# Exact-part value products and block-by-block order in the first batch of a fused attention and SwiGLU kernel

## The chip, the cores and the metric

The kernel runs on one core of one Trainium2 chip. The metric is the device time of one execution in microseconds. A profile of one execution gives the busy time of each engine, the waits, and the chain of work that ended last. PE is TensorE (matrix products), PEld its weight loads, DVE is VectorE, ACT is ScalarE, POOL is GpSimd and SP is SyncE, which issues DMA transfers here.

## The reference

Polynomial-sketch attention is followed by a SwiGLU feed-forward block. Cut to what matters:

```python
# q, k, v: (4, 4, 1088, 32); S1, S2: (8, 32)
def phi(x):
    a = np.einsum('rd,bhsd->bhsr', S1, x)
    b = np.einsum('rd,bhsd->bhsr', S2, x)
    return np.einsum('bhsi,bhsj->bhsij', a, b).reshape(*x.shape[:-1], 64)
q_p, k_p = phi(q), phi(k)
kv = np.einsum('bhsf,bhsd->bhfd', k_p, v)
z = np.sum(k_p, axis=2)
num = np.einsum('bhsf,bhfd->bhsd', q_p, kv)
den = np.einsum('bhsf,bhf->bhs', q_p, z)[..., None] + 1e-06
x = (num / den).transpose(0, 2, 1, 3).reshape(4352, 128)

# w_gate, w_val: (128, 1536); w_out: (1536, 128)
g = x @ w_gate
out = (g / (1 + np.exp(-g)) * (x @ w_val)) @ w_out
```

## The kernel before

The 4352 tokens are cut into blocks. The first batch of attention (1088 tokens) makes blocks 0, 1 and 2, of 384, 384 and 320 tokens; the rest of the tokens are in blocks of 480, and a last one of 384. The hidden dimension of 1536 is cut into 12 chunks of 128. One unit (block i, chunk j) is a gate product, a value product, and the hidden tile, silu(gate) times value. A down product then multiplies the hidden tile with a chunk of `w_out` into an accumulating bank of PSUM. The schedule is written out by hand: the order in which Python calls the helpers is the order in every engine's queue.

There are two kinds of unit. `unit` makes both products in plain fp32 (line 1015): ScalarE applies Silu to the gate bank (L1019), and VectorE multiplies with the value bank into the hidden tile (L1030). For the first six units (`late`), ScalarE only copies the value product, and the multiplication is done later by GpSimd, in `catch_up` (L1036).

`cut_unit` makes the value product, and in a later stretch the gate product too, out of parts in F32R. A weight w is cut into `w1` (w scaled by CUT and rounded to F32R, by ScalarE), `low` (w minus w1, subtracted by GpSimd or VectorE), `wb` (low times BETA, by ScalarE) and `wd` (w1 minus wb, or the same from low). Tokens are cut in the same way, into `x1`, `x0` and `xd`, by `cut_tokens` (L875, L876, L880). Three F32R products take the place of one fp32 product: wd with xd in one bank (L968), and w1 with x1 plus wb with x0 in another (L978, L979). ScalarE copies the first one to SBUF with a factor (`sums`, L972), VectorE combines it with the second bank (L980), and GpSimd multiplies the result with silu(gate) into the hidden tile (L991). Before the change only blocks from 3 on go this way; the parts of `wv` are made by `cut_weights` near the end of the first batch.

The first batch's main loop goes through `seq`, a list of 30 units; z is the position in it. At fixed positions it calls other steps:

- `parts` converts weights. The weights come as 64-bit words, and `narrow` turns each piece of three chunks into fp32 in three steps: step 1 on VectorE (L256, L257), step 2 on ScalarE (L261, L262), step 3 on VectorE (L264, L270) and GpSimd (the product in L279). Piece 3 is chunks 6 to 8 and piece 4 chunks 9 to 11. For piece 4 step 3 of `wg` is at z=8 and that of `wv` at z=10. The four pieces of `wo` have step 3 at z=14, 16, 20 and 22.
- From z=17 on, each position also has one down product (L1060) and one step of the generator `attentions`, which prepares the second batch of attention: transposes of keys and queries, key products (L347), key features (L370), the sums of features on GpSimd (`feature_sums`, L540, issued at z=24), and at z=26 `values`: the key values (L381) and a product of ones with the feature sums (L713).
- At z=24, 25 and 26 `catch_up` multiplies the last three late units.

PSUM has eight banks. Units take single banks in turn from `free_banks`, four at first, and three from z=17 on, since one accumulates the down products. A plain unit takes two banks. Hidden tiles go to `slots`: 27 tiles of 384 columns, in `hbuf` (17) and `late` (10). A down product gives its slot back. After the first batch `hbuf` is divided anew, into 13 slots of 480 columns; the rest of `late` serves for parts of the gate weights and for key features.

After the loop the remaining down products follow, with the rest of the second batch's attention among them; then the numerators (L776) and the second loop, over y, with blocks from 3 on.

Of the kernel before, what the change touches and what calls it, by code (L numbers as in the profile page):

```python
# [7 lines left out]
FP32 = mybir.dt.float32  # L8
# [11 lines left out]
def kernel(  # L20
# [279 lines left out]

    NH = 27
    NL = 10
    hbuf = const.tile([P, NH - NL, BW], FP32, name="hbuf")
    late = const.tile([P, NL, BW], FP32, tag="late", name="late", bufs=1)
    slots = [(hbuf[:, k, :] if k < NH - NL else late[:, k - NH + NL, :]) for k in range(NH)]
    slot_of = {}

    xT = const.tile([P, NT], FP32, name="xT")  # L310
# [297 lines left out]
    def attentions():  # L608
# [28 lines left out]
            f()  # L637
        yield from turn_keys(2)
        kvz = wide("a")
        values(kvz[:, 0, :], phk, zs)  # L640
        kab, kcopies = sketched(wide("b"), key_products, 2, "kab2")
        fold(kvz[:, 0, :])
        spread = spread_out(1, kvz[:, 0, :])
        hold("a", "b")
# [21 lines left out]
        for b in (2, 3):  # L666
            yield "pe"
            if b == 3:
                numerators(2, spread)
            hold("a")  # L670
            kv = bank()
            kv_bank = [max(used, key=used.get)]
            release("a")
            values(kv, phk, zs)
            if b == 2:
                kab, copies = sketched(wide("a"), key_products, 2, "kab2")
                run_copies(copies, 2)
            fold(kv)
            spread = spread_out(b, kv)
            touch(*kv_bank)  # L680
            yield
            yield "pe"
            qab, copies = sketched(wide("b"), query_sketches, 3, "qab")
            run_copies(copies, 2)
            yield
            if b == 2:
                yield from turn_queries(3)
                phk = late[:, NL - 6 :, :].rearrange("p s (n h i j) -> p (s n) h i j", h=1, i=R, j=R)
# [20 lines left out]
    def values(kv, phk, zs):  # L709

        key_values(kv[:, 0:F], phk, 0, NC)
        for h in range(H):
# [105 lines left out]
    def homes(w):  # L818


        if w is wv:
            for c in range(4):
                yield [
                    stage.tile([P, 3, P], F32R, tag=tag, name=name, bufs=6)[:]
                    for tag, name in (("exp", "w1"), ("man", "wb"), (("exp", "man")[c % 2], "wd"))
                ]
        else:
            big = lambda pool, tag, bufs: pool.tile([P, 2, 3, P], F32R, tag=tag, name="g" + tag, bufs=bufs)
            for c in range(2):
                t = [big(stage, "raw", NRAW), big(stage, "raw", NRAW), big(apool, "phq", 2)]  # L830
                for k in range(2):
                    yield [x[:, k] for x in t]

    def cut_weights(w, lows, engine):

        rows = [], [], [], []
        sub = dict(op=ALU.subtract)
        for c, (w1, wb, wd) in enumerate(homes(w)):
            src = w[:, 3 * c : 3 * c + 3, :]
            low = lows[c]  # L840
            w_parts[id(w), c] = (w1, wb, wd)
            fine = dict(out=wd, in0=whole(w1), in1=whole(wb), **sub), engine.tensor_tensor
            if engine is nc.vector:
                fine = dict(
                    out=wd, in0=low, scalar=-BETA, in1=whole(w1), op0=ALU.mult, op1=ALU.add
                ), engine.scalar_tensor_tensor
            for row, f, args in zip(
                rows,
                (nc.scalar.activation, engine.tensor_tensor, nc.scalar.activation, fine[1]),
                (  # L850
                    dict(out=w1, in_=src, func=AF.Copy, scale=CUT),
                    dict(out=low, in0=src, in1=whole(w1), **sub),
                    dict(out=wb, in_=low, func=AF.Copy, scale=BETA),
                    fine[0],
                ),
            ):
                row.append((f, args))
        return rows

    def take(steps, n):  # L860

        for _ in range(n):
            if steps:
                f, args = steps.pop(0)
                f(**args)

    def cut_tokens(i, engine=nc.gpsimd):

# [404 lines left out]
            parts.setdefault(at, []).append(p)  # L1273
    seq = [(0, 3), (0, 4), (0, 5), (2, 0), (2, 1), (2, 2)]
    seq += [(i, j) for i in (1, 2) for j in range(3, 6)]
    seq += [(i, j) for j0 in (6, 9) for i in range(3) for j in range(j0, j0 + 3)]
    order = [(i, j) for i in range(3) for j in range(NCH)]
    for z, (i, j) in enumerate(seq):
        if z == 17:
            free_banks.pop()  # L1280
            turn[0] %= 4
        unit(i, j)
        for p in parts.get(z, ()):
            part(*p)
        if z in (24, 25, 26):
            catch_up()
        if z == 6:
            load_k(1)
# [2 lines left out]
        if z >= 17:  # L1291
            todo.remove(order[0])
            todo.insert(0, order.pop(0))
            down()
        if z == 20:
            lows = [
                pool.tile([P, 3, P], FP32, tag=tag, name="low", bufs=bufs)[:]
                for pool, tag, bufs in ((apool, "qb", 2), (apool, "dT", 2), (apool, "rd", 2), (apool, "qb", 2))
            ]
            first, low, second, third = cut_weights(wv, lows, nc.gpsimd)  # L1300
        if z in (20, 21):
            take(first, 2)
        if z == 21:
            take(low, 3)
        if z == 25:
            take(second, 3)
        if z >= 17:
            parts_of(1)
        if z == 26:
            take(low, 1)  # L1310
            take(third, 3)
        if z == 29:
            take(second, 1)
            take(third, 1)
    todo.sort()
    x_steps = None
    while todo:
# [7 lines left out]
        parts_of(1)  # L1325
    run(x_steps or cut_tokens(HEAD, nc.vector))

    flat = hbuf[:].rearrange("p s w -> p (s w)")
    slots[:] = [flat[:, WB * k : WB * k + WB] for k in range((NH - NL) * BW // WB)]

# [13 lines left out]
    gate_rows = []  # L1344
    down_steps = cut_down()
    for y in range(END):
        i, j = line[y // NCH], y % NCH
# [1 line left out]
            group()  # L1349
        if y == GATES:  # L1350
            hold("g2")
        if y == END - 1:
            finish()
            unit(i, j)
        else:
            cut_unit(i, j, both=y >= GATES, y=y)
# [3 lines left out]
                down(y)  # L1360
        parts_of(y < GATES or y % 2 == 0)
        if y == 0:
            gate_rows = cut_weights(wg, lows, nc.vector)
        for n, row in enumerate(gate_rows):
            if y >= (0, 2, 6, 6)[n]:
                take(row, 1)
        for gen in token_steps.get(y, ()):
            next(gen, None)
        if y in range(24, 38, 2):
# [44 lines left out]
```

## Time and profile before

| | before |
|---|---|
| device time, median of 3 runs | 285.89 us (285.68 to 286.83) |
| span of the profile | 283.9 us, 5583 instructions |
| granted TensorE clock | 1.00 |
| HBM read and written | 11.41 and 2.23 MB |

The profile's shares by stretch, from the windows view (busy us of each engine):

| stretch, us | length | PE | DVE | ACT | POOL | what runs |
|---|---|---|---|---|---|---|
| 26.5 to 36.6 | 10.1 | 10.10 | 9.24 | 5.48 | 5.22 | z=0 to 7 |
| 36.6 to 49.5 | 12.9 | 12.90 | 10.69 | 7.99 | 3.10 | z=8 to 17 |
| 49.5 to 63.4 | 13.9 | 13.90 | 11.70 | 7.20 | 7.06 | z=18 to 23 |
| 63.4 to 77.5 | 14.1 | 14.10 | 7.09 | 5.57 | 10.82 | z=24 to 29 |
| 77.5 to 93.2 | 15.7 | 15.24 | 11.82 | 1.30 | 1.36 | down products, query features |

A busy time of PE is that of matmul records, whose ends are modelled and which overlap, so it says when TensorE had something in work and not how fast it went. For that the starts of successive matmuls in the timeline are read. The times of a line with "<-" are idle time of that engine just before the operation, and what ended it.

### The profile page before, as it was taken

What the parts mean: (1) busy time and instruction counts of PE and PEld (TensorE: products, weight loads), DVE (VectorE), ACT (ScalarE), POOL (GpSimd) and SP (SyncE); (2) the same over time, 40 slices, a digit from 0 to 9 for tenths busy, and PEclk for the clock granted to TensorE, in tenths of its full rate; (3) what the DMA queues carried; (4) which work ended last, traced back from release to release, by engine and by line L of the source; (5) the groups of instructions that cost most, each with busy time, mean ns of one, the idle gap of its engine ahead of it and who ended that gap; (6) DMA issues with size and microseconds to landing.
All of it is one profiled execution on the core that took longest, in us unless ns stands there. A gap on an engine that the chain in (4) does not pass through costs nothing.

```text
span 283.9 us, 5583 instructions
## 1 busy us (share of the span) xinstructions
PE 276.7 (97%) x2129; PEld 190.9 (67%) x2129; DVE 221.0 (78%) x324; ACT 175.5 (62%) x316; POOL 177.3 (62%) x173
## 2 busy tenths in 40 slices
PE   8899999999999999999999999999999999999995
PEld 7545565666656576555576677657777777778984
DVE  3997988975495986999648898749889969988741
ACT  3558665633401756645366777867888888977850
POOL 3314432279500896489935787659889889878660
PEclk9999999999999999999999999999999999999999
DMA  7574193222231123000100020001000200010021
GB/s 196 156 225 111 48 288 124 81 78 81 67 56 28 27 89 86 2 0 11 28 16 0 0 36 2 0 2 27 8 0 1 37 0 0 11 27 1 0 34 28
DMA packets 26138, 14.28 MB, mean 50 GB/s; under 512 B 19840, under 2 KB 24192, under 8 KB 26112
## 3 DMA queue, kind: packets, MB, share of 16 engines
q1 hardware_dynamic: 25456, 13.84, 18.7%
q8 instruction: 16, 0.26, 0.4%
q10 hardware_dynamic: 656, 0.10, 0.2%
q14 instruction: 10, 0.08, 0.1%
HBM read 11.41 MB, written 2.23 MB: 48 GB/s over the span
## 4 chain that ended last, share of the span: by engine, by line
PE 86%; DVE 6%; DMA 3%; ACT 2%; issue 1%; SPq 0%; DVEq 0%; ACTq 0%
PE PS L1060 24%; PE PS L1015 16%; PE PS L968 11%; PE PS L978 10%; PE PS L979 10%; PE PS L970 5%; DMA vld<-in_v_dram 2%; PE PS L776 2%; PE PS L335 2%; DMA raw<-in_moe_w_val_dram 1%; PE PS L347 1%; DVE sum L980 1%; PE PS L1088 1%; PE PS L1055 1%; PE PS L1052 1%
## 5 line engine op out<-in xcount | busy, mean ns | idle before, releaser
L991 POOL TENSOR_TENSOR hbuf<-sg,sum 128x480 f32<-128x480 f32 (+1 forms) x83 | 104.9, 1269 | 36.9 <-ACT sg L986 29.3
L980 DVE SCALAR_TENSOR_TENSOR sum<-PS,sum 128x960 f32<-128x960 f32 (+2 forms) x83 | 83.3, 1004 | 27.7 <-ACT sum L972 21.6
L972 ACT ACTIVATE sum<-PS 128x960 f32<-128x960 f32 (+2 forms) x83 | 70.9, 854 | 39.3 <-PE PS L968 37.9
L1060 PE MATMUL PS<-hbuf,wo 128*128 128x480 f32 (+3 forms) x142 | 57.5, 505 | 0.0
L968 PE MATMUL PS<-xd,gphq 128*128 128x480 f32 (+1 forms) x63 | 40.0, 636 | 0.5 <-DVE xd L880 0.5
L978 PE MATMUL PS<-x,w 128*128 128x480 f32 (+1 forms) x83 | 38.5, 464 | 0.0
L986 ACT ACTIVATE sg<-sum 128x480 f32<-128x480 f32 (+1 forms) x63 | 36.6, 581 | 1.0 <-DVE sum L980 0.9
L968 PE MATMUL PS<-xd,wd 128*128 128x480 f32 (+1 forms) x83 | 35.8, 432 | 0.5 <-DVE xd L880 0.5
L1060 PEld LDWEIGHTS PS<-hbuf,wo 128*128 128x128 f32 x142 | 26.6, 189 | 8.4 <-issue 0.9
L979 PE MATMUL PS<-x,wb 128*128 128x480 f32 (+1 forms) x83 | 31.2, 376 | 0.0
L1015 PE MATMUL PS<-xT,wg 128*128 128x384 f32 (+1 forms) x74 | 29.5, 480 | 0.1
L1015 PE MATMUL PS<-xT,wv 128*128 128x384 f32 (+1 forms) x74 | 28.8, 471 | 0.2 <-DVE wv L279 0.2
L1019 ACT ACTIVATE sg<-PS 128x384 f32<-128x384 f32 (+1 forms) x31 | 14.4, 467 | 21.3 <-PE PS L1015 19.6
L968 PEld LDWEIGHTS PS<-xd,wd 128*128 128x128 f32 x83 | 15.7, 189 | 13.1 <-issue 11.8
L978 PE MATMUL PS<-x,graw 128*128 128x480 f32 (+1 forms) x63 | 23.5, 373 | 0.2 <-ACT xT L793 0.2
L979 PE MATMUL PS<-x,graw 128*128 128x480 f32 (+1 forms) x63 | 23.3, 370 | 0.0
L1060 PE MATMUL PS<-hbuf,scaled 128*128 128x480 f32 x48 | 23.2, 564 | 0.0
L1015 PEld LDWEIGHTS PS<-xT,wv 128*128 128x128 f32 x74 | 13.8, 190 | 9.2 <-DVE hbuf L1030 0.9
L968 PEld LDWEIGHTS PS<-xd,gphq 128*128 128x128 f32 x63 | 11.9, 188 | 11.7 <-issue 6.8
L1015 PEld LDWEIGHTS PS<-xT,wg 128*128 128x128 f32 x74 | 13.3, 189 | 9.4 <-issue 1.3
L978 PEld LDWEIGHTS PS<-x,w 128*128 128x128 f32 x83 | 15.6, 188 | 5.8 <-issue 3.4
L979 PEld LDWEIGHTS PS<-x,wb 128*128 128x128 f32 x83 | 15.6, 188 | 5.7 <-issue 4.3
(173 smaller groups left out, 457.6 us busy)
## 6 DMA issues: line engine op xcount, KB each, us to landing
kld<-in_k_dram SPq DMA_DIRECT2D x4, 544.0 KB, 4.1
vld<-in_v_dram SPq DMA_DIRECT2D x12, 144.0 KB, 4.8
qld<-in_q_dram SPq DMA_DIRECT2D x3, 544.0 KB, 3.3
raw<-in_moe_w_out_dram SPq DMA_DIRECT2D x4, 384.0 KB, 3.7
raw<-in_moe_w_gate_dram SPq DMA_DIRECT2D x3, 384.0 KB, 3.2
raw<-in_moe_w_val_dram SPq DMA_DIRECT2D x3, 384.0 KB, 3.6
out_dram<-o SPq DMA_DIRECT2D x16, 60.0 KB, 2.0
vld<-in_v_dram SPq DMA_DIRECT2D x4, 112.0 KB, 4.5
```

Of the source, the lines that this page charges most:

```text
L335: nc.tensor.matmul(ps[32 * a : 32 * a + 32, 96 * (c - c0) : 96 * (c - c0) + 96], qT[:, 4 * c + a, :], s123[:, a : a + H, :, :].rearrange(" ...
L968: nc.tensor.matmul(ds[:, k], wd, xd, start=True, stop=True)
L970: nc.tensor.matmul(g, wg[:, j, :], xT[:, t0 : t0 + n], start=True, stop=True)
L972: nc.scalar.activation(sums, ds, AF.Copy, scale=-1.0 / BETA)
L978: nc.tensor.matmul(ps[:, k], w1, x1, start=True, stop=False)
L979: nc.tensor.matmul(ps[:, k], wb, x0, start=False, stop=True)
L980: nc.vector.scalar_tensor_tensor(out=sums, in0=ps, scalar=1.0 + 1.0 / BETA, in1=sums, op0=ALU.mult, op1=ALU.add)
L986: nc.scalar.activation(sg, sums[:, 0] if both else g, AF.Silu)
L991: nc.gpsimd.tensor_tensor(out=hj[:, 0:n], in0=sg, in1=sums[:, len(ws) - 1], op=ALU.mult)
L1015: nc.tensor.matmul(o[:, 0:n], w[:, j, :], xT[:, t0 : t0 + n], start=True, stop=True)
L1019: nc.scalar.activation(sg[:, 0:n], g[:, 0:n], AF.Silu)
L1060: nc.tensor.matmul(acc[i][:, 0:n], w, hidden[i, j][:, 0:n], **sides)
```

## The change

From chunk 6 on the three blocks of the first batch are gone through one after the other (block 0's chunks 6 to 11, then block 1's, then block 2's), instead of three chunks of each block in turn. The twelve units of blocks 1 and 2 (z=18 to 29) then become cut units, whose value products are made of exact parts[...].

For that the parts of `wv`'s chunks 6 to 11 are made at z=11 to 16 instead of from z=20 on, and those of chunks 0 to 5 at z=20 to 27; the tokens of blocks 1 and 2 are cut at z=13 to 19. The three late catch-ups move from z=24 to 26 to z=8 to 10. `cut_weights` with its rows becomes `cut_chunk`, a generator for one group of three chunks. The parts find room in other tiles; the slots go from 27 to 24, in three tiles, of which `more` also holds the key features of the third batch and gives slots back to the second loop from y=20 on. After the first batch `hbuf` has 11 slots of 480 columns. In the second batch's attention `values` is split, so that the key products of the next batch come ahead of the product with the feature sums.

The core of the diff:

```diff
-    NH = 27
+    NH = 24
     NL = 10
     hbuf = const.tile([P, NH - NL, BW], FP32, name="hbuf")
-    late = const.tile([P, NL, BW], FP32, tag="late", name="late", bufs=1)
-    slots = [(hbuf[:, k, :] if k < NH - NL else late[:, k - NH + NL, :]) for k in range(NH)]
+    late = const.tile([P, 4, BW], FP32, tag="late", name="late", bufs=1)
+    more = const.tile([P, NL - 4, BW], FP32, name="more")
+    slots = [t[:, k, :] for t, n in ((hbuf, NH - NL), (late, 4), (more, NL - 4)) for k in range(n)]
...
         kvz = wide("a")
-        values(kvz[:, 0, :], phk, zs)
+        key_values(kvz[:, 0, 0:F], phk, 0, NC)
         kab, kcopies = sketched(wide("b"), key_products, 2, "kab2")
+        value_sums(kvz[:, 0, :], zs)
         fold(kvz[:, 0, :])
...
+    def cut_chunk(w, home, low, engine):
+
+        c, (w1, wb, wd) = home
+        src = w[:, 3 * c : 3 * c + 3, :]
+        nc.scalar.activation(w1, src, AF.Copy, scale=CUT)
+        yield
+        engine.tensor_tensor(out=low, in0=src, in1=whole(w1), op=ALU.subtract)
+        yield
+        nc.scalar.activation(wb, low, AF.Copy, scale=BETA)
+        yield
+        if engine is nc.vector:
+            engine.scalar_tensor_tensor(
+                out=wd, in0=low, scalar=-BETA, in1=whole(w1), op0=ALU.mult, op1=ALU.add
+            )
+        else:
+            engine.tensor_tensor(out=wd, in0=whole(w1), in1=whole(wb), op=ALU.subtract)
+        w_parts[id(w), c] = w1, wb, wd
+        yield
...
-    seq += [(i, j) for j0 in (6, 9) for i in range(3) for j in range(j0, j0 + 3)]
+    seq += [(i, j) for i in range(3) for j in range(6, NCH)]
...
+    CUTS = 18
...
     for z, (i, j) in enumerate(seq):
         if z == 17:
             free_banks.pop()
             turn[0] %= 4
-        unit(i, j)
+        if z == CUTS:
+            turn[0] = 1
+        if z < CUTS:
+            unit(i, j)
+        else:
+            cut_unit(i, j)
         for p in parts.get(z, ()):
             part(*p)
-        if z in (24, 25, 26):
+        if z in (8, 9, 10):
             catch_up()
...
+        if z == 11:
+            give(cut_chunk(wv, next(home_v), room_for(fpool, "o", 2), nc.gpsimd), 11, 12, 14, 15)
+            give(cut_chunk(wv, next(home_v), room_for(fpool, "o", 2), nc.gpsimd), 12, 13, 15, 16)
+            give(cut_tokens(1), 13, 15)
+            give(cut_tokens(2), 16, 19)
         if z == 20:
...
+            lows = [room_for(fpool, "o", 2) for _ in range(2)]
+            give(cut_chunk(wv, next(home_v), lows[0], nc.gpsimd), 20, 21, 25, 26)
+            give(cut_chunk(wv, next(home_v), lows[1], nc.gpsimd), 21, 22, 26, 27)
         if z >= 17:
             parts_of(1)
...
+        for gen in steps_at.get(z, ()):
+            next(gen, None)
```

The first of the two chunk groups that are cut at z=11 holds chunks 9 to 11, the second chunks 6 to 8. The numbers behind each `give` are the positions of the generator's successive steps.

More of the change, by code (lines that the diff above doesn't have):

```diff
@@ L687, in attentions @@
                 yield from turn_queries(3)
-                phk = late[:, NL - 6 :, :].rearrange("p s (n h i j) -> p (s n) h i j", h=1, i=R, j=R)
+                phk = more[:].rearrange("p s (n h i j) -> p (s n) h i j", h=1, i=R, j=R)
                 phk = phk.rearrange("p (c h) o i j -> p c (h o) i j", h=H)
@@ L711, in values, with value_sums @@
         key_values(kv[:, 0:F], phk, 0, NC)
+        value_sums(kv, zs)
+    def value_sums(kv, zs):
         for h in range(H):
@@ L818, in homes @@
     def homes(w):
+        room = lambda tag, bufs: lambda: stage.tile([P, 3, P], F32R, tag=tag, name="w" + tag, bufs=bufs)[:]
+        big = lambda pool, tag, bufs: pool.tile([P, 2, 3, P], F32R, tag=tag, name="w" + tag, bufs=bufs)
+        exp, man = room("exp", 6), room("man", 6)
         if w is wv:
[L822 to L826, printed above, removed]
-        else:
[L828 to L865, printed above, removed]
+            x, y = (big(apool, "phq", 2) for _ in range(2))
+            yield 3, [x[:, 0], x[:, 1], y[:, 0]]
+            x = const.tile([P, 3, 3, P], F32R, name="w2")
+            yield 2, [x[:, k] for k in range(3)]
+            yield 0, [exp(), man(), exp()]
+            yield 1, [exp(), man(), man()]
+        else:
+            for c in range(NCH // 3):
+                x = big(stage, "raw", NRAW)
+                yield c, [x[:, 0], x[:, 1], (exp, man)[c % 2]()]
@@ L1275, with give @@
     seq += [(i, j) for i in (1, 2) for j in range(3, 6)]
-    seq += [(i, j) for j0 in (6, 9) for i in range(3) for j in range(j0, j0 + 3)]
+    seq += [(i, j) for i in range(3) for j in range(6, NCH)]
     order = [(i, j) for i in range(3) for j in range(NCH)]
+    home_v = homes(wv)
+    room_for = lambda pool, tag, bufs: pool.tile([P, 3, P], FP32, tag=tag, name="low", bufs=bufs)[:]
+    CUTS = 18
+    steps_at = {}
+    def give(gen, *at):
+        for z in at:
+            steps_at.setdefault(z, []).append(gen)
     for z, (i, j) in enumerate(seq):
@@ L1294 @@
             down()
-        if z == 20:
[L1296 to L1306, printed above, removed]
+        if z == 11:
[3 more added lines that the diff above has]
+            give(cut_tokens(2), 16, 19)
+        if z == 20:
+            lows = [room_for(fpool, "o", 2) for _ in range(2)]
+            give(cut_chunk(wv, next(home_v), lows[0], nc.gpsimd), 20, 21, 25, 26)
+            give(cut_chunk(wv, next(home_v), lows[1], nc.gpsimd), 21, 22, 26, 27)
         if z >= 17:
             parts_of(1)
[L1309 to L1314, printed above, removed]
+        for gen in steps_at.get(z, ()):
+            next(gen, None)
     todo.sort()
@@ L1326, with wide_slots @@
     run(x_steps or cut_tokens(HEAD, nc.vector))
-    flat = hbuf[:].rearrange("p s w -> p (s w)")
-    slots[:] = [flat[:, WB * k : WB * k + WB] for k in range((NH - NL) * BW // WB)]
+    def wide_slots(t, n):
+        flat = t[:].rearrange("p s w -> p (s w)")
+        return [flat[:, WB * k : WB * k + WB] for k in range(n * BW // WB)]
+    slots[:] = wide_slots(hbuf, NH - NL)
     END = len(line) * NCH
@@ L1343 @@
     lows = [late[:, c, :].rearrange("p (c f) -> p c f", f=P) for c in range(4)]
-    gate_rows = []
+    gate_steps = []
     down_steps = cut_down()
@@ L1351 @@
             hold("g2")
+            slots += wide_slots(more, NL - 4)
         if y == END - 1:
@@ L1362 @@
         if y == 0:
[L1363 to L1366, printed above, removed]
+            gate_steps = [cut_chunk(wg, h, low, nc.vector) for h, low in zip(homes(wg), lows)]
+        for k, gen in enumerate(gate_steps):
+            for at in (0, 2, 6, 6):
+                if y == at + k:
+                    next(gen)
         for gen in token_steps.get(y, ()):
```

## The prediction

> **What bounds the kernel now.** I read the page first, then the chain of waits, then the timelines of all engines between 26 and 96 us, where the change lies.
>
> ```profile
> PE 276.7 (97%) x2129; PEld 190.9 (67%) x2129; DVE 221.0 (78%) x324; ACT 175.5 (62%) x316; POOL 177.3 (62%) x173
> PE 86%; DVE 6%; DMA 3%; ACT 2%; issue 1%; SPq 0%; DVEq 0%; ACTq 0%
> ```
>
> TensorE sets the time: 86% of the chain that ended last. A busy share of 97% alone would not prove it, so I looked at its timeline around the changed stretch:
>
> ```profile
> 46.26 0.81 PE L1015 MATMUL PS<-xT,wg 128*128 128x384 f32 x2
> 46.91 0.81 PE L1015 MATMUL PS<-xT,wv 128*128 128x384 f32 x2
> 47.55 0.81 PE L1015 MATMUL PS<-xT,wg 128*128 128x384 f32 x2
> 48.20 0.81 PE L1015 MATMUL PS<-xT,wv 128*128 128x384 f32 x2
> 48.84 0.81 PE L1060 MATMUL PS<-hbuf,wo 128*128 128x384 f32 x2
> 49.48 0.70 PE L1015 MATMUL PS<-xT,wg 128*128 128x320 f32 x2
> ```
>
> A 128x384 fp32 product starts every 0.645 us (two records), a 128x320 one every 0.54, with no gaps. Counting from 26.54 us (list position z=0), z=8 starts at 36.6, z=11 at 40.0, z=12 at 41.1, z=18 at 49.5, and z=29 with its down product ends at 77.3. So TensorE has no idle to recover here: only less TensorE work helps, and any new wait is paid in full.
>
> Next, who else is near the limit. GpSimd:
>
> ```profile
> 39.71 1.00 POOL L279 TENSOR_TENSOR wg<-man,exp 128x384 f32<-128x384 f32 x1 [3.77 <-DVE man L270]
> 41.80 1.00 POOL L279 TENSOR_TENSOR wv<-man,exp 128x384 f32<-128x384 f32 x1 [1.09 <-DVE man L270]
> 46.81 1.00 POOL L279 TENSOR_TENSOR wo<-man,exp 128x384 f32<-128x384 f32 x1 [4.02 <-DVE man L270]
> 49.39 1.00 POOL L279 TENSOR_TENSOR wo<-man,exp 128x384 f32<-128x384 f32 x1 [1.58 <-DVE man L270]
> 67.75 0.73 POOL L540 TENSOR_TENSOR zs<-zs,phk 128x256 f32<-128x256 f32 x1
> ```
>
> Until 49 us it is mostly idle, waiting for VectorE. But each 384-wide operation takes about 1.0 us (3 in 2.92), and its key sums end at 68.48, just ahead of the products that read them at 68.78. ScalarE and VectorE at the same place:
>
> ```profile
> 41.95 0.49 ACT L1019 ACTIVATE sg<-PS 128x384 f32<-128x384 f32 x1 [0.75 <-PE PS L1015]
> 44.13 0.51 ACT L262 ACTIVATE man<-man 128x384 f32<-128x384 int32 x1
> 44.54 0.48 ACT L1019 ACTIVATE sg<-PS 128x384 f32<-128x384 f32 x1
> 47.82 0.56 DVE L1030 TENSOR_TENSOR late<-sg,PS 128x384 f32<-128x384 f32 x1 [0.62 <-PE PS L1015]
> 48.29 0.55 DVE L264 SCALAR_TENSOR_TENSOR exp<-raw,exp 128x384 int32<-128x384 int32 x1
> 48.76 0.55 DVE L270 SCALAR_TENSOR_TENSOR man<-raw,man 128x384 f32<-128x384 uint32 x1
> ```
>
> ScalarE starts an operation about every 0.41 us when it has work, and follows TensorE within 0.3 us.
>
> **What the Trainium skill says.** "PSUM — Partial Sum Buffer", section Engine vs sequencer instructions: the ScalarE, VectorE and GpSimd queues are strict FIFO and matmuls start in program order. The trace agrees: the catch-up at 62.07, the key sums at 63.03 and the next catch-ups at 68.45 stand in program order. "SBUF — State Buffer", section Who interferes with whom: a VectorE instruction with two SBUF inputs contends with a GpSimd one that reads SBUF. It fits: L865 on VectorE, 128x384, took 1.25 us at 99.39, when GpSimd had begun at 99.01; at 104.28 it came first and took 0.55, and GpSimd's x of 104.33 took 1.57 against its mean of 1.37. "Perfetto Trace Analysis", section Matmuls: independent groups should rotate through different PSUM banks so that the evacuation overlaps; after the change a cut unit uses each of its three banks once, so nothing is spare.
>
> **Part 1: the products of exact parts (removes TensorE work).** The F32R price at 384 comes from the last block, where a down product of 0.43 and six part products repeat every 1.48 us: 0.175 each. Three are 0.525 against 0.645, a gain of 0.12. At 320 I scale to 0.146; three are 0.44 against 0.54, a gain of 0.10. Six units of each: **-1.3 us**. That is the whole credit.
>
> **Part 2: earlier GpSimd and ScalarE work at z=8 to 17.** Three catch-ups move to z=8, 9, 10. In GpSimd's queue the wg product of z=8 still runs at 39.71 to 40.7; two catch-ups follow to 42.65, then the wv product of chunks 9 to 11, ending at 43.6 instead of 42.8. At z=11 ScalarE gets the w1 scaling of exactly these chunks. It comes up at about 41.2 and waits there until 43.6, and behind it in the queue stand the Silus. Silu of z=12 starts at 44.05 instead of 41.95 and ends at 44.55. Its PSUM bank is what the gate product of z=14 writes (four banks, two per unit): that starts at 44.6 instead of 43.68. **0.9 us lost**.
>
> ScalarE can't catch up: from 44.05 on it has the Silus of z=12 to 17 (6 x 0.39), one w1, two x1, two wb (5 x 0.41) and four weight-conversion steps (1.85 in all), together 6.2 us, to 50.2. The unit of z=17 writes the bank that Silu of z=16 (end about 49.85) frees, so its value product ends at 50.55 and the down product at 51.2, instead of 49.48. In all **1.7 us** by now.
>
> **Part 3: the first cut unit (z=18) waits for wd of chunks 6 to 8.** The wd subtraction is GpSimd's at z=16, behind the wo product of z=16, which waits for VectorE. VectorE: product of z=15 at 49.05 to 49.5 (after its Silu), then the new xd of block 1 (0.6 free, 1.17 in the trace's only 384-wide case), product of z=16 to about 51.1, then L264 and L270, to 52.1. GpSimd: wo product to 53.1, wd to **54.1**. TensorE is ready at 51.2 and waits about **2.9 us**. Bounds: if ScalarE's delay didn't exist, GpSimd alone has twelve operations from 39.71 (two weight products, three catch-ups, two lows, x0, two wo products, two wd) at 0.97 to 1.0, hence 51.4 or later, and z=18 would still be 2.0 us late. With both contended values at their worst it is 54.6.
>
> **Part 4: z=18 to 29.** A 384-wide cut unit with its down product takes 1.82 us. ScalarE gets the copy of the difference product (about 0.48, the price of a 384-wide Silu) beside the Silu: hidden, save while weights are converted. VectorE's L980 costs about what L1030 did (0.64 at 480 columns against 0.55 at 384). But its output bank is rewritten 1.5 us after it is filled, and VectorE's queue at z=19 to 23 also holds the conversions of wo, xd of block 2, query transposes and key features: I work out a wait of 0.4 us at z=24, between 0 and 1.8. GpSimd gets 12 products (1.04 and about 0.87, row L991), x0 (1.0) and two lows, together with wo's two: its queue reaches the key sums at about 69.4 and ends them (5.45 us in the trace, 63.03 to 68.48) at 74.8. TensorE, after z=26 and the split-off key values and key products, comes to the sums' product at 73.6. Wait **1.2 us**; 0 to 2.5. The split itself saves only because it puts 1.2 us of key products ahead of that wait.
>
> **Part 5: order, slots, homes.** Block-by-block order changes no work. A slot freed at z is written a unit later, in order after its down product: no wait. In the second batch 11 wide slots instead of 13 stand against at most six or seven outstanding: hidden. The split of `late`, other homes of the parts, and the generators for wg keep the same steps at the same positions: nothing. The last stretch (24 down products hiding VectorE's query features, which end at 85.25 before the numerators at 86.63) shifts as a whole.
>
> **Sum:** 1.7 + 2.9 - 1.3 + 0.4 + 1.2 = +4.9. I take 0.3 off, since a later z=18 lets GpSimd drain ahead: 285.9 + 4.6 = **290.5 us**.
>
> **Rivals.** (A) Only GpSimd's twelve operations delay z=18, by 2.0, ScalarE's block costs nothing more, and later waits are 0.5: 285.9 + 2.0 - 1.3 + 0.5 = 287.1. For it: GpSimd's count is firm; against it: ScalarE's queue order and the single Silu bank. (B) All is hidden, only part 1 counts: 284.6, the other side. For it: between 36.6 and 49.5 us the windows view has ScalarE busy for 8.0 and GpSimd for 3.1 of 12.9 us; against it: the late operand is read by the very next matmul, and TensorE has no slack. (C) VectorE stalls the single output bank and GpSimd's key sums come later still, as in the upper bounds: 285.9 + 4.9 + 1.4 + 0.8 = 293.0, since one of these waits partly hides the other.
>
> **How the numbers follow.** Forecast as worked out 0.55; (A) 0.2; (B) 0.1; (C) 0.15. The range runs from between (A) and (B), 286.2, to (C), 293.0. The band of 0.5% is 284.5 to 287.3. (B) lies near its lower edge: with a little relief elsewhere it is faster, 0.07, else no change; half of (A) falls inside the band, and the other half is slower.
>
> **What would show it.** In the changed kernel: ScalarE's w1 at about 41 us waits for GpSimd's wv product; TensorE shows a wait of about 1 us near z=14, and one of 2 to 3 us before the first F32R product, released by the GpSimd wd; GpSimd runs nearly solid from 40 to 54; the product of ones with the key sums waits for L540. F32R products of 384 columns starting about 0.175 apart confirm part 1. If the first F32R product starts by 50 us, parts 2 and 3 are wrong, and with them the forecast.

## The result, and the profile after

| | before | after |
|---|---|---|
| device time, median | 285.88 us (285.68 to 286.83) | 296.57 us (295.85 to 296.96) |
| span of the profile | 283.9 us | 294.0 us |
| granted TensorE clock | 1.00 | 0.994 |

The changed kernel is slower: the ratio of the times is 1.0364 (95% interval 1.0331 to 1.0397), or 10.7 us. The profiled execution is the fastest of its four (295.85 us); two others, at 296.92 and 296.96 us, had a lower granted clock, 0.987. The direction was foreseen. The size was not: 290.5 us was predicted, and 296.57 lies above the upper end of the range, 293.0. Lines after the edit have other numbers: the plain products are L1009, Silu is L1013, VectorE's hidden product L1024, `catch_up` L1030, the down product L1054, wd with xd L962, its copy by ScalarE L966, w1 with x1 L972, VectorE's combination L974; w1, low, wb and wd are made in L846, L848, L850 and L857, and the key sums in L541.

The chain that ended last, from the page of the kernel after:

```profile
PE 78%; DVE 9%; POOL 5%; issue 2%; ACT 2%; DMA 1%; SPq 0%; DVEq 0%; ACTq 0%; POOLq 0%
```

TensorE's share of the chain fell from 86% to 78%, and GpSimd, which had none, has 5%. TensorE's timeline, with the start, the duration, and at the right the wait and who ended it:

```profile
43.84 0.91 PE L1009 MATMUL PS<-xT,wv 128*128 128x384 f32 x2 [0.60 <-DVE late L1024]
45.45 0.91 PE L1009 MATMUL PS<-xT,wg 128*128 128x384 f32 x2 [0.70 <-ACT sg L1013]
48.27 0.88 PE L1009 MATMUL PS<-xT,wv 128*128 128x384 f32 x2 [0.61 <-DVE more L1024]
52.31 0.81 PE L1054 MATMUL PS<-hbuf,wo 128*128 128x384 f32 x2
55.91 0.44 PE L962 MATMUL PS<-xd,w 128*128 128x384 f32 x1 [2.79 <-POOL w L857]
58.57 1.09 PE L962 MATMUL PS<-xd,w 128*128 128x384 f32 x1
61.01 0.63 PE L962 MATMUL PS<-xd,w 128*128 128x384 f32 x1
64.51 0.45 PE L972 MATMUL PS<-x,wphq 128*128 128x384 f32 x1 [0.41 <-DVE sum L974]
72.79 0.42 PE L972 MATMUL PS<-x,w 128*128 128x320 f32 x1 [1.31 <-DVE sum L974]
80.45 0.32 PE L719 MATMUL PS<-zs,ones 128*32 128x64 f32 x8 [0.85 <-POOL zs L541]
```

Before the change, the down product of z=17 began at 48.84; here it begins at 52.31, so three waits and slow steps between 43 and 52 us have cost 3.5 us. Then TensorE stands for 2.95 us (52.96 to 55.91, with 0.645 us for the down product; 2.79 by the modelled end of its record) until GpSimd has made wd, and the first two cut units take 2.66 and 2.44 us (from 55.91 to 58.57 to 61.01). The numerators start 10.2 us later than before. TensorE's timelines, before and then after:

```profile
86.63 1.57 PE L776 MATMUL PS<-phT,spread 32*32 32x288 f32 x64
```

```profile
96.83 1.57 PE L782 MATMUL PS<-phT,spread 32*32 32x288 f32 x64
```

From there to the end of the profile the two kernels take the same time, 197.3 and 197.2 us. What the profiled execution lost, it lost ahead of the numerators.

Why the stretch before 52 us is late, from the timelines of VectorE, GpSimd and ScalarE of the kernel after:

```profile
40.73 1.38 DVE L264 SCALAR_TENSOR_TENSOR exp<-raw,exp 128x384 int32<-128x384 int32 x1
42.04 1.35 DVE L270 SCALAR_TENSOR_TENSOR man<-raw,man 128x384 f32<-128x384 uint32 x1
```

```profile
40.70 2.27 POOL L1030 TENSOR_TENSOR hbuf<-hbuf,sum 128x384 f32<-128x384 f32 x2
43.47 1.00 POOL L279 TENSOR_TENSOR wv<-man,exp 128x384 f32<-128x384 f32 x1 [0.49 <-DVE man L270]
54.87 0.99 POOL L857 TENSOR_TENSOR w<-w 128x384 fp32r<-128x384 f32 x1
```

```profile
44.49 0.52 ACT L846 ACTIVATE wphq<-wv 128x384 fp32r<-128x384 f32 x1 [3.26 <-POOL wv L279]
44.92 0.47 ACT L1013 ACTIVATE sg<-PS 128x384 f32<-128x384 f32 x1
```

While GpSimd makes two catch-ups (40.70 to 42.97), VectorE's two conversion steps for wv take 1.38 and 1.35 us. In the kernel before, where GpSimd is idle at that point, the same two take 0.55. GpSimd's wv product waits for them (0.49 us) and ends at 44.47; ScalarE's w1 waits for that product, and the Silu behind it in the queue starts at 44.92. VectorE's own hidden product (L1024) behind the conversions comes late too, at 43.31, and the TensorE waits at 43.84 and 45.45 are for exactly these two operations. The third wait, at 48.27, is for the L1024 that stands behind VectorE's L257 of 46.51; this L257 took 1.15 us, beside a `low` subtraction of GpSimd (46.34 to 47.45).

The slow cut units, from the windows view of the kernel after. The columns are the stretch, its length, the busy time and count of PE, PEld, DVE, ACT and POOL, then the granted TensorE clock, the DMA share and GB/s:

```profile
56.00:57.00 1.00, 1.00 (x4) 0.72 (x4) 0.00 (x0) 0.49 (x1) 0.68 (x1) 0.72 0.00 0
57.00:58.00 1.00, 1.00 (x4) 0.78 (x3) 0.00 (x0) 0.49 (x1) 0.00 (x0) 0.50 0.00 0
58.00:59.00 1.00, 1.00 (x4) 0.54 (x2) 0.82 (x3) 0.00 (x0) 0.12 (x1) 0.50 0.00 0
59.00:60.00 1.00, 1.00 (x4) 0.68 (x3) 1.00 (x1) 0.30 (x1) 0.88 (x1) 0.57 0.00 0
```

Half a microsecond after the pause the granted clock falls to one half. In windows of 0.05 us the half clock runs from 56.44 to 59.85, or 3.4 us, in which 1.7 us of full-speed work are lost. So the pause is paid for twice: once while TensorE stands, and once more while it runs slowly. Nothing of the second cost was in the prediction.

### The profile page after: what moved, and what is told of

Same layout as the page of the kernel before. It is cut to its first block, busy times and chain, and to the rows that moved or that the text cites. A ratio compares the mean times of both kernels' runs of the same rounds, so it can differ in the third digit from the quotient of the medians.

```text
span 294.0 us, 5655 instructions
## 1 busy us (share of the span) xinstructions
PE 279.5 (95%) x2141; PEld 192.6 (66%) x2141; DVE 227.2 (77%) x326; ACT 181.0 (62%) x330; POOL 191.7 (65%) x187
## 4 chain that ended last, share of the span: by engine, by line
PE 78%; DVE 9%; POOL 5%; issue 2%; ACT 2%; DMA 1%; SPq 0%; DVEq 0%; ACTq 0%; POOLq 0%
PE PS L1054 22%; PE PS L962 11%; PE PS L972 11%; PE PS L973 10%; PE PS L1009 7%; PE PS L964 6%; POOL zs L541 3%; PE PS L782 2%; PE PS L336 2%; DMA kld<-in_k_dram 1%; DVE man L270 1%; DVE sum L974 1%; PE PS L348 1%; DVE phk L371 1%; PE PS L1082 1%
## 5 line engine op out<-in xcount | busy, mean ns | idle before, releaser
L974 DVE SCALAR_TENSOR_TENSOR sum<-PS,sum 128x960 f32<-128x960 f32 (+4 forms) x95 | 89.4, 942 | 36.4 <-ACT sum L966 21.7
L985 POOL TENSOR_TENSOR hbuf<-sg,sum 128x480 f32<-128x480 f32 (+1 forms) x73 | 91.7, 1262 | 38.1 <-ACT sg L980 24.6
L966 ACT ACTIVATE sum<-PS 128x960 f32<-128x960 f32 (+4 forms) x95 | 76.4, 804 | 52.8 <-PE PS L962 50.9
L1054 PE MATMUL PS<-hbuf,wo 128*128 128x480 f32 (+3 forms) x122 | 50.0, 515 | 0.0
L985 POOL TENSOR_TENSOR more<-sg,sum 128x480 f32<-128x480 f32 (+2 forms) x22 | 25.3, 1150 | 9.1 <-ACT sg L980 5.0
L964 PE MATMUL PS<-xT,wg 128*128 128x480 f32 (+2 forms) x64 | 29.0, 535 | 0.0
L962 PE MATMUL PS<-xd,wexp 128*128 128x480 f32 (+1 forms) x52 | 26.3, 553 | 0.9 <-DVE xd L874 0.9
L1054 PEld LDWEIGHTS PS<-hbuf,wo 128*128 128x128 f32 x122 | 23.0, 191 | 6.2 <-issue 0.4
L962 PE MATMUL PS<-xd,wman 128*128 128x480 f32 (+1 forms) x53 | 27.0, 555 | 0.0
L972 PE MATMUL PS<-x,wraw 128*128 128x480 f32 (+1 forms) x63 | 23.6, 375 | 0.2 <-ACT xT L799 0.2
L973 PE MATMUL PS<-x,wraw 128*128 128x480 f32 (+1 forms) x63 | 23.5, 373 | 0.0
L1009 PE MATMUL PS<-xT,wv 128*128 128x384 f32 (+1 forms) x50 | 20.0, 482 | 1.5 <-DVE more L1024 0.6
L1009 PE MATMUL PS<-xT,wg 128*128 128x384 f32 (+1 forms) x50 | 20.4, 490 | 0.9 <-ACT sg L1013 0.8
L980 ACT ACTIVATE sg<-PS 128x480 f32<-128x480 f32 (+2 forms) x32 | 17.0, 531 | 7.0 <-PE PS L964 6.0
L972 PE MATMUL PS<-x,wexp 128*128 128x480 f32 (+1 forms) x42 | 20.2, 480 | 0.0
L962 PEld LDWEIGHTS PS<-xd,wexp 128*128 128x128 f32 x52 | 9.7, 189 | 10.4 <-issue 7.3
L1054 PE MATMUL PS<-hbuf,scaled 128*128 128x480 f32 x34 | 16.4, 564 | 0.0
L973 PE MATMUL PS<-x,wman 128*128 128x480 f32 (+1 forms) x42 | 15.7, 374 | 0.0
L962 PE MATMUL PS<-xd,w 128*128 128x480 f32 (+2 forms) x27 | 13.0, 483 | 2.8 <-POOL w L857 2.8
L962 PEld LDWEIGHTS PS<-xd,wman 128*128 128x128 f32 x53 | 9.9, 189 | 8.5 <-issue 6.6
```

What stands on the lines that cost most here:

```text
L962: nc.tensor.matmul(ds[:, k], wd, xd, start=True, stop=True)
L964: nc.tensor.matmul(g, wg[:, j, :], xT[:, t0 : t0 + n], start=True, stop=True)
L966: nc.scalar.activation(sums, ds, AF.Copy, scale=-1.0 / BETA)
L972: nc.tensor.matmul(ps[:, k], w1, x1, start=True, stop=False)
L973: nc.tensor.matmul(ps[:, k], wb, x0, start=False, stop=True)
L974: nc.vector.scalar_tensor_tensor(out=sums, in0=ps, scalar=1.0 + 1.0 / BETA, in1=sums, op0=ALU.mult, op1=ALU.add)
```

## The experiments

The kernel before was run beside them; its medians there were 286.02 (e1 to e4), 285.92 (e5 to e8) and 286.07 us (e9 to e11). Ratios are against it. The traces start up to 1.5 us apart. Where a difference between two of them is said to be aligned, both are counted from the start of the first L1009 (L1015 before the change, L1011 in e6, e7 and e11), which is at 15.12 us before and 15.16 after.

**e1: catch-ups three positions earlier.** Are the catch-ups, at z=8 to 10, what delays ScalarE?

```diff
-        if z in (8, 9, 10):
+        if z in (5, 6, 7):
             catch_up()
```

> The changed kernel with the three catch-ups at z=5, 6 and 7, where GpSimd has nothing to do, instead of z=8, 9 and 10. Theory (the catch-ups delay the wv product of z=10, both as work ahead of it in GpSimd's queue and by making VectorE's L264 and L270 of z=10 take 1.38 and 1.35 us instead of 0.55): L264 and L270 back at about 0.55, the wv product ends near 42.8 instead of 44.4, the w1 of chunks 9 to 11 starts near 42.8, and TensorE ends the down product of z=17 about 1.5 to 2.5 us earlier than 52.96; the first F32R product starts near 54, and the time falls by 1.5 to 2.5 us to about 294.5. Rival (the number of operations on ScalarE and GpSimd between z=11 and 17 sets z=18 whatever comes before): under 0.5 us less.

Measured: 295.12 us, ratio 1.0316 (1.0289 to 1.0342). The wv product did end earlier, at 44.25, or 0.5 us aligned. But the catch-ups, now at 36.18 to 39.33, slowed the conversions that stand there instead. GpSimd's and VectorE's timelines in e1:

```profile
36.18 3.15 POOL L1030 TENSOR_TENSOR hbuf<-hbuf,sum 128x384 f32<-128x384 f32 x3
```

```profile
36.30 1.08 DVE L256 TENSOR_SCALAR exp<-raw 128x384 int32<-128x384 int32 x1
37.31 1.16 DVE L257 TENSOR_SCALAR man<-raw 128x384 int32<-128x384 int32 x1
```

Where GpSimd is idle, L256 and L257 take 0.35 us each, as in the kernel before:

```profile
36.30 0.36 DVE L257 TENSOR_SCALAR man<-raw 128x384 int32<-128x384 int32 x1
```

Aligned, TensorE was 0.9 us late already at z=12, its down product of z=17 began only 0.7 us earlier than in the changed kernel, and the pause before the first F32R product stayed at 2.79 us. In the profiled execution the clock didn't fall after this pause, in the three others it did (0.994, 0.994, 0.992), so part of the 1.45 us can be the clock's. The expectation was missed: a free place in GpSimd's queue is not enough, what runs beside the catch-ups counts.

**e2: TensorE kept busy in the pause.** Thirteen dummy bf16 products, which no one reads, are put in ahead of the first cut unit.

```diff
         if z == CUTS:
             turn[0] = 1
+            keep_warm(13)
```

> The changed kernel with 13 dummy bf16 products of 512 columns ([...]written to the bank that the first F32R product then overwrites) between the down product of z=17 and z=18, in the 2.95 us in which TensorE waits. Nothing else is changed. Theory (TensorE's clock falls to half because TensorE stood idle for 2.8 us): the granted clock stays 1.00 in the next 5 us, the first two cut units take 1.82 us each instead of 2.66 and 2.44, and the time falls by 1.5 us to about 295.1. Rival (the first F32R products are slow for another reason, or the clock drop comes from the profile's own doing): those units stay at 2.4 to 2.7 us and the time stays at 296.6.

Measured: 294.85 us, ratio 1.0305 (1.0281 to 1.0328), as expected: 1.7 us less than the changed kernel, with a clock of 0.999 or 1.0 in every run. TensorE's timeline in e2:

```profile
52.90 3.00 PE L234 MATMUL PS<-const-bfloat16-1.0 128*32 128x512 bf16 x13
55.83 0.44 PE L962 MATMUL PS<-xd,w 128*128 128x384 f32 x1
57.46 0.63 PE L962 MATMUL PS<-xd,w 128*128 128x384 f32 x1
59.27 0.63 PE L962 MATMUL PS<-xd,w 128*128 128x384 f32 x1
```

The first F32R product starts where it did (55.83, after 55.91), but the first two cut units take 1.63 and 1.81 us. In the changed kernel they took 5.10 together, here 3.44. The half clock is a cost of its own, 1.66 us here, and the standing still causes it. By the numerators 1.0 us of this gain is left (aligned), since TensorE's waits for VectorE's L974 grew from 1.7 to 2.2 us. The medians differ by more, 1.7 us, because two executions of the changed kernel took longer, at a clock of 0.987: one half-clock stretch of 3.4 us brings the mean of such a run to about 0.994, two to about 0.988. Where a second one fell, no trace shows.

**e3: plain products, the cutting left in.** All parts are made as in the changed kernel, but nothing reads them in the first batch.

```diff
-        if z < CUTS:
-            unit(i, j)
-        else:
-            cut_unit(i, j)
+        unit(i, j)
```

> The changed kernel with plain fp32 units at z=18 to 29 too; all parts are still cut at the same positions (those of chunks 6 to 8 and 9 to 11 and of blocks 1 and 2's tokens are then used by nothing in the first batch). It pays for the cutting before z=18 and has neither the wait for wd, nor the single PSUM bank per purpose, nor twelve more GpSimd products. Theory (3.5 us are lost before z=18, the other 6.7 us come from the wait for wd, the clock after it, VectorE's single output bank and the key sums, less 1.3 gained): 285.9 + 3.5 = 289.4, between 288.8 and 290.5. Rival (order, slots and homes cost too): above 291.

Measured: 289.72 us, ratio 1.0126 (1.0102 to 1.015), as expected. The three waits before z=18 are still there (0.6, 0.7 and 0.6 us), no wait for wd, for L974 or for the key sums is left. So 3.7 us come without any cut unit: from making the parts and the moved catch-ups, with the new order, slots and homes of parts, which this run keeps too. The other 6.9 us come with the cut units, which were to save 1.3.

**e4: the order alone.** The kernel before, with the list gone through block by block.

```diff
-    seq += [(i, j) for j0 in (6, 9) for i in range(3) for j in range(j0, j0 + 3)]
+    seq += [(i, j) for i in range(3) for j in range(6, NCH)]
```

> The kernel before with the block-by-block order of units from chunk 6 on, and nothing else. Theory: the order alone costs nothing, 285.9 within 0.5. Rival (order and the earlier down products collide with weights not yet converted): over 287.

Measured: 286.48 us, ratio 1.0024 (1.0011 to 1.0037). A wait for the key sums of 0.2 us appears. Aligned, the down product of z=17 begins when it did before, and the numerators 0.45 us later. The order costs 0.5 us, which the prediction had put at nothing.

**e5: wd ahead of the wo product at z=16.** GpSimd makes the wd subtractions before it queues for VectorE.

```diff
+        if z == 16:
+            for gen in steps_at.pop(16):
+                next(gen, None)
         for p in parts.get(z, ()):
             part(*p)
```

> The changed kernel with the part steps of z=16 (wd of chunks 6 to 8 and x1, x0 of block 2) issued ahead of the conversion of wo at z=16, so that GpSimd does the wd of chunks 6 to 8 before the wo product that waits for VectorE. Theory (the wd is late because it stands behind that product): wd ends near 53.9 instead of 55.86, TensorE's pause before the first F32R product falls from 2.95 to about 1.0 us, the clock then stays at 1.00, and the time is 1.9 + up to 1.6 us less: 293.0 to 294.7. Rival (GpSimd's queue is full, so the order in it doesn't matter): 296.0 or more.

Measured: 293.28 us, ratio 1.0244 (1.0205 to 1.0282). The wait for wd in the list of TensorE's waits, in e5:

```profile
PE PS L962 <- POOL w L857: 1.2, 1, 1.2
```

The wait shrinks from 2.79 to 1.16 us, or by 1.6, and the clock stays at 0.999 or above in every run. That leaves 1.7 of the 3.3 us gained, as much as e2 gained with the pause filled and not shortened. The expectation held, and with it the prediction's reason for the wait: the wd stood behind a product that waits for VectorE.

**e6: a second bank.** Is VectorE's L974 late because its bank is the only one? From e2, every other cut unit from z=19 to 25 puts its second group into another bank. (VectorE's L974 is L976 in this run, and GpSimd's L985 is L987.)

```diff
+        if aside:
+            ps = bank("b")[:, 0:n].unsqueeze(1)
...
-            cut_unit(i, j)
+            cut_unit(i, j, aside=z in (19, 21, 23, 25))
```

> The kernel with the 13 dummy products (294.85 us), whose cut units at z=19, 21, 23 and 25 put the products of w1 and wb into a bank that is idle then (bank 6), so that VectorE's L974 has two banks in turn up to z=25. Theory (two waits of together 2.2 us, the longer 1.3, arise because one bank is refilled before VectorE, which is behind, has read it): both fall under 0.3 us; the wait for the key sums grows from 0.9 to 1.5 to 3 us, since GpSimd's queue doesn't get shorter; the time falls by 0.3 to 1.5 us, to 293.4 to 294.5. Rival (VectorE is simply too slow, so the wait comes back at the next bank): waits for L974 of 1.5 us or more stay.

Measured: 296.36 us, ratio 1.035 (1.0316 to 1.0384), 1.5 us more than e2. The waits for VectorE did fall, from 2.2 to 1.0 us. TensorE then came to the key sums earlier and waited there longer. Its timeline and the windows view in e6:

```profile
79.68 0.32 PE L719 MATMUL PS<-zs,ones 128*32 128x64 f32 x8 [2.40 <-POOL zs L541]
```

```profile
80.00:85.00 5.00, 5.00 (x81) 3.39 (x80) 1.87 (x5) 1.41 (x3) 4.05 (x5) 0.66 0.08 16
```

The 1.2 us saved became 1.5 us more of the next wait, and this pause of 2.4 us brought the half clock back: a mean of 0.66 over these 5 us. The longer wait, of 1.5 to 3 us, had been expected. The expectation was missed because it left out the clock, and because only one of the two waits for VectorE went with the second bank: 0.96 us stayed, one unit later.

**e7: the later subtractions behind the key sums.** From e6, GpSimd's `low` of chunks 0 to 5 moves from z=21 and 22 to z=24.

```diff
-            give(cut_chunk(wv, next(home_v), lows[0], nc.gpsimd), 20, 21, 25, 26)
-            give(cut_chunk(wv, next(home_v), lows[1], nc.gpsimd), 21, 22, 26, 27)
+            give(cut_chunk(wv, next(home_v), lows[0], nc.gpsimd), 20, 24, 27, 28)
+            give(cut_chunk(wv, next(home_v), lows[1], nc.gpsimd), 21, 24, 27, 29)
```

> The kernel of the second bank, with the two low subtractions of chunks 0 to 5 moved in GpSimd's queue from z=21 and 22 to z=24, behind the key sums, and their wb and wd to z=27 to 29. Theory (GpSimd's queue of products, lows and wo conversions ahead of the key sums sets the wait of the product of ones): the key sums end about 2 us earlier, TensorE's wait for them goes to under 0.7 us, and the time falls by another 1 to 2 us, to 292 to 293.3. Rival (the key sums start late because VectorE's key features are late): the wait changes by under 0.5 us.

Measured: 295.31 us, ratio 1.03 (1.0257 to 1.0342), and still 1.9 us of wait for the key sums: missed. Aligned, the key sums did end 1.7 us earlier than in e6, but TensorE came to them 1.2 us earlier too, because its last wait for VectorE is gone. VectorE's timeline in e6, then in e7:

```profile
67.83 1.27 DVE L264 SCALAR_TENSOR_TENSOR exp<-raw,exp 128x384 int32<-128x384 int32 x1
```

```profile
67.57 0.53 DVE L264 SCALAR_TENSOR_TENSOR exp<-raw,exp 128x384 int32<-128x384 int32 x1
```

With the L270 behind it, this conversion of `wo` takes 2.6 us in e6, beside a `low` and a product of GpSimd, and 1.0 us in e7, where the `low` has moved away. So it was the slowed conversions that kept a wait for VectorE alive beside the second bank. One execution kept the full clock and took 293.62 us; the three others had 0.994 and took 295.26 to 295.45. The same program, then, pays for a lower clock in some executions and not in others.

**e8: only block 2 cut, with the parts made at z=18 to 25.** Its six cut units should save 6 x 0.10 = 0.6 us, and the crowded stretch before z=18 is left alone. Blocks 0 and 1 are plain; the catch-ups come at z=25 to 27.

```diff
-    CUTS = 18
+    CUTS = 24
...
-        if z in (8, 9, 10):
+        if z in (25, 26, 27):
             catch_up()
...
-        if z == 11:
-            give(cut_chunk(wv, next(home_v), room_for(fpool, "o", 2), nc.gpsimd), 11, 12, 14, 15)
-            give(cut_chunk(wv, next(home_v), room_for(fpool, "o", 2), nc.gpsimd), 12, 13, 15, 16)
-            give(cut_tokens(1), 13, 15)
-            give(cut_tokens(2), 16, 19)
+        if z == 18:
+            give(cut_chunk(wv, next(home_v), room_for(fpool, "o", 2), nc.gpsimd), 19, 20, 22, 25)
+            give(cut_chunk(wv, next(home_v), room_for(fpool, "o", 2), nc.gpsimd), 18, 19, 21, 22)
+            give(cut_tokens(2), 20, 22)
```

> The changed kernel with cut units in block 2 only (z=24 to 29): block 1 keeps plain units and its tokens are not cut, the parts of chunks 6 to 11 are cut at z=18 to 25, the catch-ups stand at z=25 to 27, and the parts of chunks 0 to 5 at z=24 to 29, behind the key sums. Nothing is added on GpSimd or ScalarE before z=18. Theory (the price is where the cutting stands: z=8 to 17 leave VectorE and ScalarE no room, z=18 to 23 leave some): no pause before z=18, and the time is 285.9 - 0.6 + 0 to 1.5 us of waits at z=18 to 26, between 285.3 and 287. Rival (cut units of the first batch can't be fed in any position): above 288.

Measured: 292.92 us, ratio 1.0233 (1.0193 to 1.0274): missed. Before z=18 there was no wait, but TensorE then waited 1.5 us for xd, 0.9 for the key sums, and 2.4 for the wd of chunks 9 to 11, which GpSimd had behind the key sums. The half clock followed the last of these. The number is the rival's, but its reason, that no position feeds the cut units, is refuted by e10. A position where an engine has time on average doesn't help when a long operation of the same queue stands ahead.

**e9: e5, with the catch-ups at z=18 to 20.** This separates the catch-ups from the cutting.

```diff
-        if z in (8, 9, 10):
+        if z in (18, 19, 20):
             catch_up()
```

> The kernel with the wd ahead of the wo product (293.28 us), with the three catch-ups at z=18, 19 and 20 instead of 8, 9 and 10. Moving them to z=5, 6, 7 had won under 1 us, since there they slowed VectorE's L256 and L257 instead. Theory (the catch-ups, wherever they stand before z=18, are what VectorE and ScalarE have no room for): L264 and L270 of z=10 at 0.55 to 0.8, the waits of 0.6 and 0.7 us at z=13 and 14 go, the first F32R product starts 2.5 to 3.5 us earlier than 54.1, and the time is 290 to 291. Rival (the parts of two chunk groups and two token blocks are too much by themselves before z=18): less than 1.2 us, above 292.1.

Measured: 291.97 us, ratio 1.0184 (1.0133 to 1.0236), 1.3 us less than e5: missed, since 290 to 291 was expected, and close to the rival's 1.2. VectorE's timeline, then TensorE's, in e9:

```profile
40.85 0.55 DVE L264 SCALAR_TENSOR_TENSOR exp<-raw,exp 128x384 int32<-128x384 int32 x1
41.32 0.55 DVE L270 SCALAR_TENSOR_TENSOR man<-raw,man 128x384 f32<-128x384 uint32 x1
```

```profile
50.51 0.81 PE L1054 MATMUL PS<-hbuf,wo 128*128 128x384 f32 x2
52.47 0.44 PE L962 MATMUL PS<-xd,w 128*128 128x384 f32 x1 [1.15 <-POOL w L857]
```

With no catch-ups beside them the same two conversions take 0.55 us each, the wv product ends at 42.95, and the waits at z=13 and 14 are gone. The down product of z=17 begins at 50.51. Of the 3.4 us lost before it (aligned), 1.9 belong to the catch-ups, and 1.5 to the cutting itself. Of the 1.9 us gained here 0.7 go to a longer wait for the key sums, 1.54 us instead of 0.86. Neither this wait nor the one for wd, 1.15 us, lowered the clock, which stayed at 0.999 or 1.0.

**e10: e8, mended.** All parts of chunks 6 to 11 are made at z=18 to 21, the key sums are issued ahead of the unit of z=24, the catch-ups come at z=26 to 28.

```diff
+        if z == 24:
+            parts_of(1)
...
-        if z in (25, 26, 27):
+        if z in (26, 27, 28):
...
-            give(cut_chunk(wv, next(home_v), room_for(fpool, "o", 2), nc.gpsimd), 19, 20, 22, 25)
-            give(cut_chunk(wv, next(home_v), room_for(fpool, "o", 2), nc.gpsimd), 18, 19, 21, 22)
-            give(cut_tokens(2), 20, 22)
+            give(cut_chunk(wv, next(home_v), room_for(fpool, "o", 2), nc.gpsimd), 18, 19, 20, 21)
+            give(cut_chunk(wv, next(home_v), room_for(fpool, "o", 2), nc.gpsimd), 18, 19, 20, 21)
+            give(cut_tokens(2), 18, 21)
...
-        if z >= 17:
+        if z >= 17 and z != 24:
             parts_of(1)
```

> The kernel with cut units in block 2 only (292.92 us), whose three long waits of TensorE came from where I had put the steps: xd of block 2 behind key features (1.5 us), the key sums behind the first product (0.9), and wd of chunks 9 to 11 behind the key sums (2.4, and then half clock). Here the parts of chunks 6 to 11 and of block 2's tokens are all cut by z=21, the key sums are issued ahead of unit z=24, and the catch-ups stand at z=26 to 28. Theory (the cost is only in the position of the steps): no wait of TensorE over 0.5 us before the second batch, no half clock, and 285.4 to 286.6 us: the order's 0.5 less the 0.6 that six shorter value products save. Rival (there is always another queue that is full): above 287.5.

Measured: 286.31 us, ratio 0.9999 (0.9976 to 1.0022) over twelve executions. The list of TensorE's waits has none left in the first batch. The one that it has (0.5 us for xd, at 94.94) is at the start of the second loop, and the kernel before has it too. The cut units themselves are not what is slow: with their parts ready in time the six of block 2 cost nothing. Nor is anything gained, as expected. That 0.6 us of shorter products stand against the 0.5 us of the order fits this, but the interval is as wide as either.

**e11: e9 with everything found.** The second bank of e6, the late subtractions of e7 and the early key sums of e10 together.

```diff
+        if z == 24:
+            parts_of(1)
...
-            cut_unit(i, j)
+            cut_unit(i, j, aside=z in (19, 21, 23, 25))
...
-            give(cut_chunk(wv, next(home_v), lows[0], nc.gpsimd), 20, 21, 25, 26)
-            give(cut_chunk(wv, next(home_v), lows[1], nc.gpsimd), 21, 22, 26, 27)
-        if z >= 17:
+            give(cut_chunk(wv, next(home_v), lows[0], nc.gpsimd), 20, 24, 27, 28)
+            give(cut_chunk(wv, next(home_v), lows[1], nc.gpsimd), 21, 24, 27, 29)
+        if z >= 17 and z != 24:
             parts_of(1)
```

> All remedies for twelve cut units together: wd ahead of the wo product, catch-ups at z=18 to 20, bank 6 in turn for the products of w1 and wb up to z=25, the lows of chunks 0 to 5 behind the key sums, and the key sums issued ahead of unit z=24. Theory (each wait is a separate payment): from the catch-up kernel's 290 to 291, less 1 to 2 for VectorE's bank and 0.9 for the key sums, 287.5 to 289. Rival (GpSimd's queue is the bound from z=11 to the key sums, and every wait that is taken away comes back at the next place): within 0.7 us of the catch-up kernel.

Measured: 291.49 us, ratio 1.0163 (1.0102 to 1.0223), within 0.5 us of e9: missed, and what the rival had said. The waits for VectorE fell to 0.9 us, and the numerators start 1.3 us earlier than in e9 (aligned); 1.3 us of wait for the key sums and 1.2 for wd stay. In the profiled execution, the slowest of the four, TensorE keeps this lead up to its last product. Some 1.0 us is lost behind it; the last output transfers take 2.0 us to land there, and 1.5 in e9. So that every wait comes back elsewhere, as the rival has it, is not shown. No version here beats the kernel before.

## Why the prediction was wrong in size

**Part 1, the credit: right.** A cut unit and its down product start every 1.81 us in e2 (57.46 to 59.27), where 1.82 was worked out.

**Part 2, the lateness before z=18: the mechanism right, the size half.** 1.7 us was predicted and 3.5 measured, the largest error of the sum. ScalarE's w1 did wait for the wv product with the Silus behind it, and TensorE did wait near z=14 for a Silu. The failed term is the end of the wv product, 43.6, which was counted from GpSimd's queue alone with VectorE at 0.55 us per conversion; it measured 44.47. The prediction had itself quoted the Trainium skill's page "SBUF — State Buffer", section Who interferes with whom, by which a VectorE instruction with two SBUF inputs contends with a GpSimd one that reads SBUF, but left it out of Part 2. Here the moved catch-ups meet two conversions with two SBUF operands each: 1.38 and 1.35 us, against 0.55 in e9 once the catch-ups are gone. That also delays VectorE's hidden product, a TensorE wait (0.60 us) that wasn't foreseen. And e9 shows that even without the catch-ups the cutting costs 1.5 us; part of that can be the same contention (L257 took 1.15 us there at 44.72, beside GpSimd's `low` subtraction), but no run tells it from ScalarE's load, so its split stays open.

**Part 3, the wait for wd: right.** 2.9 us predicted, 2.95 measured, released by the wd subtraction, and e5 confirms the reason. The wd ended at 55.86, and not at 54.1. That the size fits so well is in part luck: TensorE and the wd both came 1.8 us later than reckoned.

**The half clock after the pause: missing.** The sum has no term for it; it cost about 1.7 us (e2). The Trainium skill's page "TensorE: Matmul & The Clock Gate", section Part 1: The HAM clock gate, gives half the clock after an idle window of some 3.4 us, in windows that run freely. The traces agree with the half clock, and it lasts 3.4 us in all three that show it (after, e6, e8). They differ in what brings it on: TensorE stood for no such window as a whole. Pauses of 2.79 us (after) and 2.4 us (e6, and e8 with one of 0.86 us shortly ahead) were enough, and the clock fell only 0.05 to 0.6 us after their end; 1.54 us (e9) was not enough. With 1.9 us one e7 execution kept the clock, with 2.79 us one of e1; that fits a window which the pause meets at a chance position, though no run here controlled it.

**Part 4: VectorE too low, the key sums right.** Waits for L974 were 0.41 and 1.31 us, together 1.7, against 0.4 (0 to 1.8 was allowed). The single bank is only part of their cause: e6, with a second one, still waits 1.0 us. The rest went in e7, when the conversions of `wo` took 1.0 us instead of 2.6, so VectorE was late there beside GpSimd, as in Part 2. The wait for the key sums was 0.85 us, against 1.2. The two are tied, as e6 shows: what was taken from the first went to the second. Rival (C) held this in its mechanism but counted neither the contention nor the clock.

**Part 5, the order: 0 predicted, 0.5 measured** (e4).

**The sum.** 3.5 + 2.95 + 1.7 + 1.7 + 0.85 - 1.3 = 9.4 us, of the 10.2 by which the numerators are late. Of the remaining 0.8 the order can be 0.5 (e4); the rest was not traced. In the prediction's sum the failed terms are Part 2 (1.8 us too low), the clock (1.7, not in the sum) and VectorE's waits (1.3 too low). The 0.3 us that the prediction took off for a GpSimd that drains meanwhile isn't seen.

Of the named signs all but one came: GpSimd was busy for 10.3 of the 14 us from 40 to 54, so it was not nearly solid. Most of its idle time was spent waiting for ScalarE and VectorE, which were late themselves.

## What to carry to other kernels

When work is moved to an idle engine, look at what its new neighbours in time do: here a stretch in which GpSimd was mostly idle was just where VectorE ran two-operand steps, and three moved operations cost 1.9 us without being late themselves. Count a pause of TensorE like those of 2.4 us and more here as possibly paid twice, since the clock may be halved after it; those of 1.2 to 1.5 us in e5 and e9 were paid once. Before a saving of 0.1 us per unit is built, make the operands of the first unit early enough that no long operation stands ahead of them in a queue: with six cut units, that decided between 292.92 us (e8) and 286.31 (e10).

## What the runs showed of the hardware that was not expected

- After pauses of 2.4 us (e6) to 2.79 us (after) the granted clock was 0.5 for 3.4 us, beginning up to 0.6 us after the pause had ended. It came in most executions and not in all: the same program (e7, with a pause of 1.9 us in the profiled execution) took 293.62 us at a clock of 1.0 and 295.26 to 295.45 us at 0.994. Dummy products in the pause prevented it in all four executions of e2.
- The contention of VectorE with GpSimd also reaches operations with a single tensor operand: L256 and L257 took 1.08 and 1.16 us beside GpSimd's catch-ups (e1), and 0.35 without. The two-operand steps took 1.35 to 1.38, and 0.55 without.
